# A streaming decode kernel: the last three K pieces moved up the load order, x added in mid-run, eight output-weight blocks in two ring slots

## The chip, the cores and the metric

One core of one Trainium2 chip. The metric is device time in microseconds of one execution. Times of one kernel agree to about 0.3 us in most runs, with a run about 1 us longer now and then. The profile is one execution, taken by the hardware profiler; its span is about 1.7 us shorter than the time of the same execution. MB of a single load are 1024 KB; totals and GB/s are in millions and billions of bytes, as the page gives them.

## The reference

For four requests (B = 4, one token each): attention over a cache of 8192 keys and values in 32 heads of 128, then the output weight `wo`; beside it a gated feed-forward layer of the same x; and a mix of both.

```python
x = A_x                                                   # (4, 1, 1024), bf16
g = sigmoid((x * gate_w).sum(-1, keepdims=True))
a = softmax((x @ wq -> heads) @ K^T / sqrt(128)) @ V @ wo  # K, V: (4, 32, 8192, 128)
b = x + (silu(x @ w_gate) * (x @ w_up)) @ w_down * sigmoid(x @ w_r)
return g * a + (1 - g) * b
```

K and V are 537 of the 576 MB that have to be read; every byte is used once.

## The kernel before

K and V come in 64 pieces each of 4 MB (two heads of one request: 128 partitions by 32 KB). Every load, of weights too, goes through a ring of five slots of 32 KB per partition. A K piece is transposed by DVE in four parts and multiplied by PE; four K pieces make a group with one softmax; V pieces are multiplied four steps later.

```python
ring = ctx.enter_context(tc.tile_pool(name="ring", bufs=5))
def slot():
    return ring.tile([P, RING], BF, name="piece", tag="piece")
# ... cut ...
def wo_piece(g0, g1, r0=0, r1=FR):                 # one wo block: 1 MB, in a slot of 4 MB
    ng, nr = g1 - g0, r1 - r0
    w = slot()[:, :ng * nr * D].rearrange("p (g r n) -> p g r n", g=ng, r=nr)
    nc.sync.dma_start(out=w..., in_=wov[:, g0:g1, r0:r1]...)
    def use(): ...                                 # 8 matmuls of 4x512 into acc
    return use
# ... cut ...
for u in range(NT + LAG):                          # NT = 64, LAG = 4
    if u < NT:
        k_piece(u)                                 # after every fourth: softmax(group)
    if u >= LAG:
        v_piece(u - LAG)                           # the last one is loaded in four parts
    if side:
        side.pop(0)()
    if u == NT:
        o_rows(0, GE)
        add_x()                                    # loads x again, adds (1 - g) * x
    if u == NT + LAG - 2:
        for g in range(2):
            wo_piece(g, g + 1)()
last = [wo_piece(g, g + 1) for g in range(2, NWB - 1)]
last += [wo_piece(NWB - 1, NWB, 0, FR - 1), wo_piece(NWB - 1, NWB, FR - 1, FR)]
flush()
o_rows(GE, NWB)
for use in last:
    use()
# ... then acc is cast by DVE and ACT, in halves, and stored
```

So the loads end with: V 62, wo0, wo1, V 63 in four parts of 1 MB, wo2 to wo6 (1 MB each), wo7 as 768 KB and 256 KB.

Of the kernel before, what the change touches and what calls it, by code (L numbers as in the profile page):

```python
# [19 lines left out]
def kernel(  # L20
# [22 lines left out]
    nc = tc.nc  # L43
    P = 128
    Bn, Sq, D = A_x.shape
# [6 lines left out]
    GT = 4  # L52
# [4 lines left out]
    NT = Bn * H // HT  # L57
    LAG = 4
    FR = 4
    FG = F // (P * FR)  # L60
    NB = 512
    NH = D // NB
# [18 lines left out]
    def slot():  # L81
        return ring.tile([P, RING], BF, name="piece", tag="piece")
# [53 lines left out]
    LT = const.tile([P, FR, H // FR, Bn], BF)  # L136
# [10 lines left out]
    acc = accp.tile([Bn, D], F32)  # L147

    def mm_acc(out_ap, lhsT, rhs, start=False):
        nc.tensor.matmul(out_ap, lhsT=lhsT, rhs=rhs, start=start, stop=True, skip_group_check=True)  # L150
# [15 lines left out]
    def add_x():  # L166
        xb = ptp.tile([Bn, D], BF, name="xb", bufs=1)
        nc.sync.dma_start(out=xb[:], in_=x2)
        xf = ptp.tile([Bn, D], F32, name="xf", bufs=1)
        nc.vector.tensor_copy(out=xf[:], in_=xb[:])  # L170
        for n in range(NH):
            mm_acc(acc[:, n * NB:(n + 1) * NB], dg[:], xf[:, n * NB:(n + 1) * NB])
# [6 lines left out]
    wov = A_wo.rearrange("(g p r) n -> p g r n", p=P, r=FR)  # L179
# [17 lines left out]
    def gu_piece(view, w_i, t0):  # L197
        w = slot()[:, :TW * F].rearrange("p (t g f r) -> p t g f r", t=TW, g=FG, r=FR)
        nc.sync.dma_start(out=w.rearrange("p t g f r -> p t (g f r)"), in_=view[:, t0:t0 + TW, :])
        for t in range(TW):  # L200
            for g in range(FG):
                for r in range(FR):
                    mm_acc(gu_ps[:, w_i, g, r, :], w[:, t, g, :, r], xT[t0 + t])

    def h_done():
        g_sb = stat.tile([P, FT, Bn], F32, tag="g_sb", bufs=1)
        fl = lambda ap: ap.rearrange("p g r b -> p (g r) b")
        nc.scalar.activation(out=g_sb[:], in_=fl(gu_ps[:, 0]), func=ACT.Silu)
        nc.vector.tensor_tensor(out=g_sb[:], in0=g_sb[:], in1=fl(gu_ps[:, 1]), op=ALU.mult)
        nc.vector.tensor_tensor(out=fl(hT[:]), in0=g_sb[:],  # L210
                                in1=c12[:, 1:2, :].to_broadcast([P, FT, Bn]), op=ALU.mult)

    def wd_piece(g0, ng):
        w = slot()[:, :ng * FR * D].rearrange("p (g r n) -> p g r n", g=ng, r=FR)
        nc.sync.dma_start(out=w.rearrange("p g r n -> p g (r n)"),
                          in_=wdv[:, g0:g0 + ng].rearrange("f g r n -> f g (r n)"))
        for g in range(ng):
            for r in range(FR):
                for n in range(NH):
                    mm_acc(acc[:, n * NB:(n + 1) * NB], hT[:, g0 + g, r, :], w[:, g, r, n * NB:(n + 1) * NB],  # L220
                           start=(g0 + g + r == 0))

    WB = P * FR // Dh
    NWB = H // WB
# [8 lines left out]
                                 rhs=OT[:, WB * g0 + k:WB * g1:WB, :], start=True, stop=True, skip_group_check=True)  # L233
        nc.vector.tensor_copy(out=LT[:, :, g0:g1, :], in_=lp[:])

    def wo_piece(g0, g1, r0=0, r1=FR):
        ng, nr = g1 - g0, r1 - r0
        w = slot()[:, :ng * nr * D].rearrange("p (g r n) -> p g r n", g=ng, r=nr)
        nc.sync.dma_start(out=w.rearrange("p g r n -> p g (r n)"),
                          in_=wov[:, g0:g1, r0:r1].rearrange("p g r n -> p g (r n)"))  # L240

        def use():
            for g in range(ng):
                for r in range(nr):
                    for n in range(NH):
                        mm_acc(acc[:, n * NB:(n + 1) * NB], LT[:, r0 + r, g0 + g, :], w[:, g, r, n * NB:(n + 1) * NB])
        return use


# [4 lines left out]
    def flush():  # L254
        while pending:
            pending.pop(0)()

    def heads(u):
        return divmod(u * HT, H)

    def kv_view(cache, u):
        b, h0 = heads(u)
        return cache[b, h0:h0 + HT].rearrange("h (r j) d -> (h r) (j d)", j=JR)

    def k_piece(u):
        b, h0 = heads(u)
        g, t = divmod(u, GT)
        Z = Zt[u % 2]
        for a in range(NQ):
            nc.gpsimd.tensor_copy(out=Z[32 * a:32 * a + 32, :, 31 + 32 * a:32 + 32 * a],  # L270
                                  in_=qa[32 * a:32 * a + 32, :, h0 + a // QH, b:b + 1])
        if t == 0:
            S_ps[g] = scp.tile([P, 512], F32, name="S_ps")
        sps = S_ps[g]
        kn = slot()
        nc.sync.dma_start(out=kn[:], in_=kv_view(A_k_cache, u))
        for c in range(JR // CJ):
            T = ttp.tile([P, CJ, 2, 32, 2], BF, name="T", tag="T")
            nc.vector.transpose(out=T[:].rearrange("p j h i e -> p (j h i e)").bitcast(U32),  # L279
                                in_=kn[:, c * CJ * Dh:(c + 1) * CJ * Dh].bitcast(U32))  # L280
            for jl in range(CJ // 16):
                jc = c * (CJ // 16) + jl
                s = 31 - (JC * t + jc)
                for he in range(4):
                    half, e = divmod(he, 2)
                    nc.tensor.matmul(sps[:, :], lhsT=Z[:, he, s:s + P], rhs=T[:, 16 * jl:16 * jl + 16, half, :, e],  # L286
                                     start=(t == 0 and jc == 0 and he == 0),
                                     stop=(t == GT - 1 and jc == JC - 1 and he == 3))
            if c == 0:
                flush()  # L290
        if t == GT - 1:
            softmax(g)
# [34 lines left out]
    def v_piece(u):  # L327
        b, h0 = heads(u)
        g, t = divmod(u, GT)
        B_ = PB[g % 2]  # L330
        vn = slot()
        vv = kv_view(A_v_cache, u)
        cut = 4 if u == NT - 1 else 1
        for c in range(cut):
            lo, hi = c * RING // cut, (c + 1) * RING // cut
            nc.sync.dma_start(out=vn[:, lo:hi], in_=vv[:, lo:hi])
        o_ps = ops.tile([P, 4 * Dh], F32, name="o_ps")
        n = 0
        for jc in range(JC):
            for uq in range(4):  # L340
                j0 = 16 * jc + 4 * uq
                nc.tensor.matmul(o_ps[32 * t:32 * t + NM, :], lhsT=B_[:, JC * t + jc, uq].rearrange("p s j -> p (s j)"),  # L342
                                 rhs=vn[:, j0 * Dh:(j0 + 4) * Dh], start=(n == 0), stop=(n == JR // 4 - 1))
                n += 1
                if n == 8:
                    flush()
        o_sb = OS[g % 2]
        nc.scalar.copy(out=o_sb[32 * t:32 * t + NM, :], in_=o_ps[32 * t:32 * t + NM, :])  # L348
        if t < GT - 1:
            return  # L350

        def finish():
            oT = o2p.tile([P, GH], F32, name="oT")
            for q in range(4):
                nc.tensor.matmul(oT[:, :], lhsT=o_sb[:, q * Dh:(q + 1) * Dh],  # L355
                                 rhs=selg[:, q].rearrange("p t s -> p (t s)"), start=(q == 0), stop=(q == 3))
            hg = h0 + HT - GH
            nc.vector.scalar_tensor_tensor(out=OT[:, hg:hg + GH, b], in0=oT[:, :], scalar=sgb[:, 1, b:b + 1],  # L358
                                           in1=rinv_t.pop(g)[:], op0=ALU.mult, op1=ALU.mult)
        pending.append(finish)  # L360
# [6 lines left out]
    side = [lambda: gu_piece(wgv, 0, 0), lambda: gu_piece(wgv, 0, TW), lambda: gu_piece(wuv, 1, 0),  # L367
            lambda: (gu_piece(wuv, 1, TW), h_done()), lambda: wd_piece(0, 4), lambda: wd_piece(4, FG - 4)]
    GE = NWB - GH // WB
    for u in range(NT + LAG):  # L370
        if u < NT:
            k_piece(u)
        if u >= LAG:
            v_piece(u - LAG)
        if side:
            side.pop(0)()
        if u == NT:
            o_rows(0, GE)
            add_x()
        if u == NT + LAG - 2:  # L380
            for g in range(2):
                wo_piece(g, g + 1)()
    last = [wo_piece(g, g + 1) for g in range(2, NWB - 1)]
    last += [wo_piece(NWB - 1, NWB, 0, FR - 1), wo_piece(NWB - 1, NWB, FR - 1, FR)]
    flush()
    o_rows(GE, NWB)
    for use in last:
# [36 lines left out]
```

## Time and profile before

| | before |
|---|---|
| median of 4 runs (lowest, highest), us | 1351.43 (1351.25, 1352.2) |
| profiled span, us | 1349.4 |
| loaded, MB | 576 |
| last landing mark of all loads, us from the span's start | 1345.19 |

The first lines of the page of the kernel before, with its queues: the span, busy time per engine, the packets, and for each queue its packets, MB, and share of the sixteen load engines' time.

```profile
span 1349.4 us, 11817 instructions
PE 1065.0 (79%) x5112; PEld 434.1 (32%) x5112; DVE 622.4 (46%) x403; ACT 71.0 (5%) x118; POOL 86.2 (6%) x326
DMA packets 22040, 576.46 MB, mean 427 GB/s; under 512 B 2386, under 2 KB 2394, under 8 KB 2660
...
q1 hardware_dynamic: 21968, 575.69, 99.4%
q8 instruction: 40, 0.66, 0.2%
```

No compute engine is near its limit, while the loads run at 427 GB/s over the whole span.

The table of stretches of the kernel before. Columns: the stretch, its length, busy time of each engine, granted PE clock, mean busy share of the load engines, GB/s.

```profile
core 0: us, PE busy (x) PEld busy (x) DVE busy (x) ACT busy (x) POOL busy (x), PEclk, DMA share, GB/s
60.00:1240.00 1180.00, 944.75 (x4230) 379.64 (x4230) 571.15 (x361) 61.20 (x103) 73.57 (x285) 0.91 1.00 431
...
1320.00:1336.00 16.00, 14.80 (x95) 6.48 (x94) 0.42 (x2) 1.15 (x2) 0.00 (x0) 1.00 1.00 408
1336.00:1340.00 4.00, 3.67 (x17) 1.36 (x16) 0.00 (x0) 0.00 (x0) 0.00 (x0) 1.00 0.85 327
1340.00:1346.00 6.00, 5.18 (x23) 1.93 (x23) 0.00 (x0) 0.00 (x0) 0.00 (x0) 1.00 0.48 194
```

For 1180 us the load engines are busy all the time. In the last ten the rate falls to less than half. The chain of waits is followed back from the end (start, us, what):

```profile
1309.47 20.69 DMA piece<-in_A_v_cache_dram
...
1330.21 1.90 PE o_ps L342 x8
...
1332.13 10.53 DMA piece<-in_A_wo_dram
...
1342.69 1.89 PE acc L150 x8
```

It says: the last V matmuls end at 1332.1, only then wo6 is issued (its slot was V 63's), it lands 10.5 us later, and the kernel ends after it. The timeline of the sync engine's queue confirms the late issues, and the list of its waits says why the last V piece was late too, and that the wo loads waited for V matmuls to free their slots (start, us, instruction; in the second fence: us in total, times, longest):

```profile
1308.15 1.75 SPq L336 DMA_DIRECT2D piece<-in_A_v_cache_dram  x4
...
1332.13 0.33 SPq L239 DMA_DIRECT2D piece<-in_A_wo_dram  x1
...
1336.24 2.06 SPq L239 DMA_DIRECT2D piece<-in_A_wo_dram  x2
```

```profile
SPq L239 <- PE o_ps L342: 23.2, 4, 8.6
...
SPq L336 <- PE o_ps L232: 12.4, 1, 12.4
```

The V matmuls of the last group were held by its softmax, on the timeline by the copy of the weights on POOL:

```profile
1299.37 8.75 PE L342 MATMUL o_ps<-piece,PB_143 128*8 128x512 bf16 x32 [2.11 <-POOL PB_143 L316]
```

When a load completes, the trace holds sixteen increments of its semaphore. The Trainium skill, page "DMA: Bandwidth & Descriptors", section "Why a DMA increments its semaphore by 16 and not by 1", explains them: each engine that takes part posts its own +1 behind its own data. So the first mark shows the engine that is furthest ahead, the last mark the one that is furthest behind, and only the last one ends the load. The following is worked out from the trace's landing records, in us (for the semaphores whose marks can be assigned to their loads without doubt):

```
kernel before    issued    first mark   last mark   spread
w_gate, 1st half   2.54       40.35       42.18      1.83
V, mid-run       701.05      734.12      739.04      4.92
V              1231.73     1258.65     1266.64      7.99
wo1            1295.51     1312.18     1320.22      8.04
V 63, part 1   1308.15     1314.67     1322.70      8.03
V 63, part 2   1308.53     1317.16     1325.18      8.02
V 63, part 3   1309.01     1319.65     1327.67      8.02
wo5            1325.77     1332.64     1340.17      7.53
wo6            1332.13     1336.48     1342.65      6.17
wo7, 768 KB    1336.24     1340.65     1344.55      3.89
wo7, 256 KB    1337.97     1341.31     1345.19      3.88
```

The engine that is last takes 2.47 to 2.57 us for each MB from 1320.22 to 1342.65 (nine MB in 22.43 us: 2.49 each), then 1.90 us for 768 KB and 0.64 us for 256 KB. There is no gap in its work: the pace is the same before and after the late issues. (The marks don't name the engines, so the last mark need not always be of the same one.) The engines that are ahead do run dry, which is the hole in the table of stretches.

### The profile page before, as it was taken

What the parts mean: (1) busy time and instruction counts of PE and PEld (TensorE: products, weight loads), DVE (VectorE), ACT (ScalarE), POOL (GpSimd) and SP (SyncE); (2) the same over time, 40 slices, a digit from 0 to 9 for tenths busy, and PEclk for the clock granted to TensorE, in tenths of its full rate; (3) what the DMA queues carried; (4) which work ended last, traced back from release to release, by engine and by line L of the source; (5) the groups of instructions that cost most, each with busy time, mean ns of one, the idle gap of its engine ahead of it and who ended that gap; (6) DMA issues with size and microseconds to landing.
All of it is one profiled execution on the core that took longest, in us unless ns stands there. A gap on an engine that the chain in (4) does not pass through costs nothing.

```text
span 1349.4 us, 11817 instructions
## 1 busy us (share of the span) xinstructions
PE 1065.0 (79%) x5112; PEld 434.1 (32%) x5112; DVE 622.4 (46%) x403; ACT 71.0 (5%) x118; POOL 86.2 (6%) x326
## 2 busy tenths in 40 slices
PE   2776887778788877868788777879778787887798
PEld 2432333233233323323333323333333333333333
DVE  1553445544544545355355535534553454455420
ACT  0001000000000000000000000000000000000000
POOL 2000000000000000000000000000000000000000
PEclk9877998989899888989989898999988889998999
DMA  9999999999999999999999999999999999999997
GB/s 402 431 433 422 432 431 430 431 432 433 430 431 432 431 428 432 434 430 428 432 434 431 428 432 434 431 429 430 434 431 428 432 434 432 429 429 434 433 421 321
DMA packets 22040, 576.46 MB, mean 427 GB/s; under 512 B 2386, under 2 KB 2394, under 8 KB 2660
## 3 DMA queue, kind: packets, MB, share of 16 engines
q1 hardware_dynamic: 21968, 575.69, 99.4%
q8 instruction: 40, 0.66, 0.2%
q14 instruction: 12, 0.10, 0.0%
q10 hardware_dynamic: 20, 0.02, 0.0%
HBM read 575.69 MB, written 0.01 MB: 427 GB/s over the span
## 4 chain that ended last, share of the span: by engine, by line
DMA 47%; PE 31%; DVE 11%; issue 8%; POOL 2%; ACT 1%; SPq 0%; DVEq 0%; ACTq 0%
DMA piece<-in_A_k_cache_dram 45%; PE o_ps L342 16%; PE S_ps L286 12%; DVE T L279 10%; DMA piece<-in_A_v_cache_dram 2%; PE oT L355 1%; PE acc L150 1%; DMA piece<-in_A_wo_dram 1%; DVE PT L311 1%; POOL PB_143 L316 1%; POOL PB_142 L316 1%; PE shr L150 1%; POOL tot L320 0%; ACT OS_138 L348 0%; ACT OS_139 L348 0%
## 5 line engine op out<-in xcount | busy, mean ns | idle before, releaser
L279 DVE STREAM_TRANSPOSE T<-piece 128x2048 uint32<-128x2048 uint32 x256 | 576.3, 2288 | 477.0 <-DMA piece<-in_A_k_cache_dram 395.1
L286 PE MATMUL S_ps<-T,Z_140 128*128 128x512 bf16 x1024 | 296.5, 447 | 169.0 <-DVE T L279 168.6
L286 PE MATMUL S_ps<-T,Z_141 128*128 128x512 bf16 x1024 | 253.6, 393 | 77.8 <-DVE T L279 77.7
L342 PE MATMUL o_ps<-piece,PB_143 128*8 128x512 bf16 x1024 | 227.1, 381 | 2.3 <-POOL PB_143 L316 2.1
L342 PE MATMUL o_ps<-piece,PB_142 128*8 128x512 bf16 x1024 | 226.2, 379 | 0.0
L286 PEld LDWEIGHTS <-Z_140 128*128 128x128 bf16 x1024 | 113.5, 111 | 347.8 <-issue 272.2
L286 PEld LDWEIGHTS <-Z_141 128*128 128x128 bf16 x1024 | 100.7, 99 | 229.5 <-issue 130.4
L342 PEld LDWEIGHTS <-PB_143 128*8 128x8 bf16 x1024 | 86.5, 87 | 139.8 <-issue 15.6
L342 PEld LDWEIGHTS <-PB_142 128*8 128x8 bf16 x1024 | 86.4, 87 | 137.3 <-issue 13.2
L358 DVE SCALAR_TENSOR_TENSOR OT<-oT,sgb,rinv 128x8 bf16<-128x8 f32 x16 | 3.8, 236 | 128.4 <-PE oT L355 128.4
L270 POOL COPY Z_140<-qa 32x4 bf16<-32x4 bf16 x128 | 24.9, 195 | 512.5 <-PE S_ps L286 497.7
L270 POOL COPY Z_141<-qa 32x4 bf16<-32x4 bf16 x128 | 24.9, 195 | 511.6 <-PE S_ps L286 506.0
L348 ACT COPY OS_138<-o_ps 8x512 f32<-8x512 f32 x32 | 18.4, 576 | 599.7 <-PE o_ps L342 599.7
L348 ACT COPY OS_139<-o_ps 8x512 f32<-8x512 f32 x32 | 18.4, 576 | 536.1 <-PE o_ps L342 536.1
L150 PE MATMUL shr<-xw,piece 128*128 128x4 bf16 x704 | 22.6, 170 | 3.5 <-DMA piece<-in_A_wq_dram 3.3
L150 PEld LDWEIGHTS <-piece 128*128 128x128 bf16 x704 | 22.6, 113 | 4.6 <-DMA piece<-in_A_wq_dram 3.4
L150 PE MATMUL acc<-piece,LT 128*4 128x512 bf16 x64 | 14.6, 378 | 1.1 <-DMA piece<-in_A_wo_dram 1.1
L322 DVE RECIPROCAL rinv<-tot 128x8 f32<-128x8 f32 x16 | 3.2, 202 | 25.5 <-POOL tot L320 25.5
L355 PE MATMUL oT<-selg,OS_139 128*128 128x8 f32 x64 | 8.5, 259 | 5.7 <-ACT OS_139 L348 5.7
L355 PE MATMUL oT<-selg,OS_138 128*128 128x8 f32 x64 | 8.5, 259 | 5.7 <-ACT OS_138 L348 5.7
L316 POOL COPY PB_143<-PT 64x512 bf16<-64x512 bf16 x8 | 8.2, 1026 | 66.0 <-DVE rex L318 66.0
L150 PE MATMUL acc<-piece,hT 128*4 128x512 bf16 x56 | 12.4, 379 | 0.0
(99 smaller groups left out, 145.1 us busy)
## 6 DMA issues: line engine op xcount, KB each, us to landing
piece<-in_A_k_cache_dram SPq DMA_DIRECT2D x64, 4096.0 KB, 37.4
piece<-in_A_v_cache_dram SPq DMA_DIRECT2D x63, 4096.0 KB, 36.5
piece<-in_A_wq_dram SPq DMA_DIRECT2D x2, 4096.0 KB, 22.8
piece<-in_B_w_gate_dram SPq DMA_DIRECT2D x2, 3584.0 KB, 39.6
piece<-in_B_w_up_dram SPq DMA_DIRECT2D x2, 3584.0 KB, 34.5
piece<-in_A_wo_dram SPq DMA_DIRECT2D x7, 1024.0 KB, 14.4
piece<-in_B_w_down_dram SPq DMA_DIRECT2D x1, 4096.0 KB, 39.4
piece<-in_A_v_cache_dram SPq DMA_DIRECT2D x4, 1024.0 KB, 16.7
```

The costliest lines, as they stand in the source:

```text
L150: nc.tensor.matmul(out_ap, lhsT=lhsT, rhs=rhs, start=start, stop=True, skip_group_check=True)
L270: nc.gpsimd.tensor_copy(out=Z[32 * a:32 * a + 32, :, 31 + 32 * a:32 + 32 * a], in_=qa[32 * a:32 * a + 32, :, h0 + a // QH, b:b + 1])
L279: nc.vector.transpose(out=T[:].rearrange("p j h i e -> p (j h i e)").bitcast(U32), in_=kn[:, c * CJ * Dh:(c + 1) * CJ * Dh].bitcast(U32))
L286: nc.tensor.matmul(sps[:, :], lhsT=Z[:, he, s:s + P], rhs=T[:, 16 * jl:16 * jl + 16, half, :, e], start=(t == 0 and jc == 0 and he == 0), ...
L311: nc.vector.transpose(out=PT[:].rearrange("p j i -> p (j i)"), in_=PTs[:])
L316: nc.gpsimd.tensor_copy(out=B_[W:P, :, :, 1, :], in_=Pv[W:P])
L322: nc.vector.reciprocal(out=rinv[:], in_=tot[:])
L342: nc.tensor.matmul(o_ps[32 * t:32 * t + NM, :], lhsT=B_[:, JC * t + jc, uq].rearrange("p s j -> p (s j)"), rhs=vn[:, j0 * Dh:(j0 + 4) * Dh ...
L348: nc.scalar.copy(out=o_sb[32 * t:32 * t + NM, :], in_=o_ps[32 * t:32 * t + NM, :])
L355: nc.tensor.matmul(oT[:, :], lhsT=o_sb[:, q * Dh:(q + 1) * Dh], rhs=selg[:, q].rearrange("p t s -> p (t s)"), start=(q == 0), stop=(q == 3))
L358: nc.vector.scalar_tensor_tensor(out=OT[:, hg:hg + GH, b], in0=oT[:, :], scalar=sgb[:, 1, b:b + 1], in1=rinv_t.pop(g)[:], op0=ALU.mult, op ...
```

## The change

Its intent: the last four K pieces are loaded in two pairs (60 with 61, 62 with 63), so the last softmax is done before the tail and the last V pieces don't wait for it; wo blocks share slots, four in each, so their loads can be issued early and the load engines never run dry; and the x load and its matmuls leave the tail.

```diff
-    def wo_piece(g0, g1, r0=0, r1=FR):
-        ...
-        w = slot()[:, :ng * nr * D]...
+    wo_home = {}
+    def wo_block(g, r0=0, r1=FR):
+        home, at = divmod(g, 4)
+        if home not in wo_home:
+            wo_home[home] = slot().rearrange("p (g r n) -> p g r n", g=4, r=FR)
+        w = wo_home[home][:, at]
         ...
-    for u in range(NT + LAG):
-        ...
+    order = []
+    for u in range(NT - GT):
+        order += [("k", u)] + [("v", u - LAG)] * (u >= LAG)
+    n0 = NT - GT - LAG
+    order += [("k", NT - 4), ("k", NT - 3), ("v", n0), ("k", NT - 2), ("k", NT - 1)]
+    order += [("v", u) for u in range(n0 + 1, NT)]
+    for kind, u in order:
+        if kind == "k":
             k_piece(u)
+        if (kind, u) == ("v", NT - 1):
+            for g in range(2):
+                wo_block(g)()
+        if kind == "v":
+            v_piece(u)
         ...
+        if (kind, u) == ("k", NT // 2):
+            add_x()
+        if (kind, u) == ("v", NT - LAG):
             o_rows(0, GE)
-            add_x()
-        if u == NT + LAG - 2: ...
+    last = [wo_block(g) for g in range(2, NWB - 1)]
+    last += [wo_block(NWB - 1, 0, FR - 1), wo_block(NWB - 1, FR - 1, FR)]
```

More of the change, by code (lines that the diff above doesn't have):

```diff
@@ L234, in o_rows @@
         nc.vector.tensor_copy(out=LT[:, :, g0:g1, :], in_=lp[:])
-    def wo_piece(g0, g1, r0=0, r1=FR):
-        ng, nr = g1 - g0, r1 - r0
-        w = slot()[:, :ng * nr * D].rearrange("p (g r n) -> p g r n", g=ng, r=nr)
-        nc.sync.dma_start(out=w.rearrange("p g r n -> p g (r n)"),
-                          in_=wov[:, g0:g1, r0:r1].rearrange("p g r n -> p g (r n)"))
+    wo_home = {}
[4 more added lines that the diff above has]
+        w = wo_home[home][:, at]
+        nc.sync.dma_start(out=w[:, r0:r1].rearrange("p r n -> p (r n)"),
+                          in_=wov[:, g, r0:r1].rearrange("p r n -> p (r n)"))
         def use():
-            for g in range(ng):
-                for r in range(nr):
-                    for n in range(NH):
-                        mm_acc(acc[:, n * NB:(n + 1) * NB], LT[:, r0 + r, g0 + g, :], w[:, g, r, n * NB:(n + 1) * NB])
+            for r in range(r0, r1):
+                for n in range(NH):
+                    mm_acc(acc[:, n * NB:(n + 1) * NB], LT[:, r, g, :], w[:, r, n * NB:(n + 1) * NB])
         return use
@@ L369 @@
     GE = NWB - GH // WB
-    for u in range(NT + LAG):
-        if u < NT:
-            k_piece(u)
-        if u >= LAG:
-            v_piece(u - LAG)
-        if side:
+    order = []
[6 more added lines that the diff above has]
+        if kind == "k":
+            k_piece(u)
+        if (kind, u) == ("v", NT - 1):
[3 more added lines that the diff above has]
+            v_piece(u)
+        if side and (kind == "v" or u < LAG):
             side.pop(0)()
-        if u == NT:
+        if (kind, u) == ("k", NT // 2):
+            add_x()
+        if (kind, u) == ("v", NT - LAG):
             o_rows(0, GE)
-            add_x()
-        if u == NT + LAG - 2:
-            for g in range(2):
-                wo_piece(g, g + 1)()
-    last = [wo_piece(g, g + 1) for g in range(2, NWB - 1)]
-    last += [wo_piece(NWB - 1, NWB, 0, FR - 1), wo_piece(NWB - 1, NWB, FR - 1, FR)]
+    last = [wo_block(g) for g in range(2, NWB - 1)]
+    last += [wo_block(NWB - 1, 0, FR - 1), wo_block(NWB - 1, FR - 1, FR)]
     flush()
```

## The prediction

> **What bounds the kernel now.** The load stream. The page gives 576.46 MB in a span of 1349.4 us; in the table of stretches the window from 60 to 1240 us has a DMA share of 1.00 at 431 GB/s, beside PE busy 945 of 1180 us and DVE 571. The Trainium skill, page "DMA: Bandwidth & Descriptors", section "Specifications", gives a fabric ceiling of 435 GB/s; the trace agrees, at 431. So only the two ends of the stream can give time back.
>
> **The tail before.** The last group's softmax ends at 1299.4 us (timeline) and holds the V matmuls that should have begun about 3.6 us sooner (their piece landed at 1295.8). That delays slot releases: the last V piece is issued at 1308.2 instead of about 12 us sooner (SP's waits: 12.4 us on PE), and the last three wo loads, each in a slot of its own, are issued only at 1332.1, 1336.2 and 1338.0. From 1336 to 1345 us only 2.5 MB move where the earlier rate would need 5.7 us: about 3 us of DMA idle. The naive forecast of the change is therefore -2 to -3 us.
>
> **Why I don't believe that.** Each transfer leaves sixteen landing marks. The same page, section "Why a DMA increments its semaphore by 16 and not by 1", says that each engine's last descriptor posts its own +1, so the spread of the marks is the spread between engines. The trace shows it: from 1.8 us at the start it grows to 8.0 us (first mark of a V piece 1258.65, last 1266.64), and stays there to 1328. What ends a load is the slowest engine. Its last marks in the tail stand at 1320.22, 1322.70, 1325.18, 1327.67, then 1340.17 (five blocks later), 1342.65, 1344.55 (768 KB) and 1345.19 (256 KB): 2.48 to 2.50 us per MB throughout, with no gap. The late issues starve only engines that are ahead: the spread shrinks to 3.9 us, while the last mark doesn't move. After it come the last matmuls (to 1346.5), the casts and the output's store: 4.2 us, unchanged.
>
> **What the change does.** Removed: the late softmax from the V stream's tail (about 10 us from the last scores to the weights, now early) and the slot waits of wo; the built order shows that wo2 and wo3, wo5 to wo7 wait for no slot. Moved: the x load (8 KB), its 0.63 us cast and four matmuls (1.9 us) go to mid-run, where PE is 80% busy. The pairs put two K pieces back to back: 4 transposes of 2.29 us, about 9.3 us with gaps, against 9.7 us per piece of stream, so the slot comes free in time; queued loads take 35 to 40 us to land, a deep reserve. Added bytes: none. On the critical path (the slowest engine's queue) lies next to nothing of all this.
>
> **Prediction.** 1351.3 us, range 1350.0 to 1352.6. Faster by over 2%: 0.005; within 2%: 0.99; slower: 0.005.
>
> **What would show it.** Right: wo6 and wo7 issued before about 1325 us; DMA in the last slices fuller; landing spread of the last wo loads near 8 us instead of 3.9, their first marks earlier and the last mark still at 1345 +-0.7 us; the V matmuls of the last group no longer released by the softmax; the stretch 60 to 1240 at 431 GB/s. Wrong: a last mark at about 1342 us (the idle was on the critical engine after all), or a gap in the last marks around the K pairs.
>
> **What would make it wrong.** A different assignment of small or instruction fetches to the slowest engine (shifts its queue by up to 1 us); PE falling behind on the doubled K pieces so that the queue drains; the last matmuls no longer hidden.

## The result and the profile after

| | before | after |
|---|---|---|
| median of 4 runs each, us | 1351.43 | 1351.24 (1351.19 to 1351.37) |
| ratio (95% interval) | | 0.9998 (0.998 to 1.0015) |
| profiled span, us | 1349.4 | 1349.5 |
| last landing mark, us | 1345.19 | 1345.28 |
| spread of the last load's marks, us | 3.88 | 7.92 |

A ratio here is the mean time of one kernel's fast runs over that of the other's of the same rounds, so it is not quite the ratio of the medians. The time is the same. (Every run below is marked correct; at the runs with left-out matmuls it is said how little that mark tells here.)

The change did in the profile what it was meant to do. The last V and wo loads are issued earlier (timeline of the sync engine's queue), and the last group's V matmuls wait for their own piece instead of the softmax:

```profile
1293.23 2.91 SPq L340 DMA_DIRECT2D piece<-in_A_v_cache_dram  x4
1305.53 22.59 SPq L244 DMA_DIRECT2D piece<-in_A_wo_dram  x7
```

```profile
1295.84 8.64 PE L346 MATMUL o_ps<-piece,PB_143 128*8 128x512 bf16 x32 [0.91 <-DMA piece<-in_A_v_cache_dram]
```

What the wo loads wait for has changed its kind: by the list of the queue's waits, most of it is now the landing of earlier loads, because the program keeps eight completion semaphores in turn and the ninth load waits for the first. wo6 was issued at 1322.81, just after the last mark of V 63's first part (1322.80).

```profile
SPq L244 <- DMA piece<-in_A_v_cache_dram: 26.4, 6, 9.5
```

The stretches after, to be read against those of before:

```profile
60.00:1240.00 1180.00, 947.14 (x4232) 379.91 (x4231) 578.63 (x364) 61.26 (x103) 73.64 (x285) 0.91 1.00 431
...
1320.00:1336.00 16.00, 14.95 (x97) 6.62 (x95) 0.43 (x2) 1.16 (x2) 0.00 (x0) 1.00 1.01 421
1336.00:1340.00 4.00, 4.00 (x21) 1.54 (x19) 0.00 (x0) 0.00 (x0) 0.00 (x0) 1.00 0.81 329
1340.00:1346.00 6.00, 5.32 (x25) 1.95 (x24) 0.00 (x0) 0.00 (x0) 0.00 (x0) 1.00 0.41 167
```

The stretch from 1320 rose from 408 to 421 GB/s: the holes of the engines in front are filled there. But they only finish sooner, and the last six microseconds are emptier than before (167 against 194 GB/s). The chain of waits has lost its V matmuls and its late issue, and still ends in the same place:

```profile
1293.23 29.56 DMA piece<-in_A_v_cache_dram
...
1322.81 19.94 DMA piece<-in_A_wo_dram
...
1342.79 3.79 PE acc L150 x16
```

wo6 now takes 19.9 us to land instead of 10.5: the issue moved by 9.3 us, the landing by 0.1. The marks, worked out as before:

```
kernel after     issued    first mark   last mark   spread
wo5            1320.34     1332.36     1340.18      7.83
wo6            1322.81     1334.85     1342.75      7.90
wo7, 768 KB    1325.30     1336.72     1344.63      7.92
wo7, 256 KB    1327.79     1337.36     1345.28      7.92
```

### The profile page after: what moved, and what is told of

Read it like the earlier page. It is cut to its first block, busy times and chain, and to the rows that moved or that the text cites. A ratio compares the mean times of both kernels' runs of the same rounds, so it can differ in the third digit from the quotient of the medians.

```text
span 1349.5 us, 11806 instructions
## 1 busy us (share of the span) xinstructions
PE 1066.2 (79%) x5112; PEld 434.1 (32%) x5112; DVE 622.5 (46%) x403; ACT 71.0 (5%) x118; POOL 86.3 (6%) x326
## 4 chain that ended last, share of the span: by engine, by line
DMA 48%; PE 32%; DVE 12%; issue 6%; POOL 2%; ACT 1%; DVEq 0%; SPq 0%; ACTq 0%
DMA piece<-in_A_k_cache_dram 42%; PE o_ps L346 16%; PE S_ps L290 14%; DVE T L283 10%; DMA piece<-in_A_v_cache_dram 5%; DMA piece<-in_A_wo_dram 1%; PE oT L359 1%; PE acc L150 1%; DVE PT L315 1%; PE shr L150 1%; POOL PB_142 L320 1%; POOL PB_143 L320 1%; POOL tot L324 0%; ACT OS_138 L352 0%; ACT OS_139 L352 0%
## 5 line engine op out<-in xcount | busy, mean ns | idle before, releaser
L313 ACT ACTIVATE PTs<-S_ps,negm 128x512 bf16<-128x512 f32 x16 | 11.0, 688 | 25.8 <-DVE negm L310 25.4
## 6 DMA issues: line engine op xcount, KB each, us to landing
piece<-in_A_wo_dram SPq DMA_DIRECT2D x7, 1024.0 KB, 19.9
```

The costliest lines, as they stand in the source:

```text
L313: nc.scalar.activation(out=PTs[:], in_=sps[:], func=ACT.Exp, bias=negm[:, 0:1], scale=scale, accum_out=rs[:, 0:1])
```

## The experiments

Theory A: the load engine with the longest queue is never idle, so the time is set by what that one engine has to move; earlier issue feeds engines that were not the limit. Rivals: B, the earlier issue does gain and another part of the change takes it back; C, the issue of the last loads sets the end, as the chain of waits seems to say; D, the spread of the engines is of no matter. A second theory, A2, came up on the way: what makes some engines late is the fetching of PE's own instructions. Its rivals: E, fetches don't matter; F, PE's time itself counts. Times and ratios are set against the kernel before, which ran again in each round (median 1351.23 or 1351.26), landing marks against the changed kernel.

### Shared slots alone

```diff
 # the kernel before, with wo_piece(g, g + 1) replaced by
+ wo_block(g)          # as in the change; order of pieces and add_x untouched
```

> The kernel before with the shared wo slots alone; K order and the x load as before. Theory A (the load engine with the longest queue never idles, so earlier issue gains nothing): 1351.3 +-0.4 us, last landing mark at 1345.2 +-0.5, spread of the last wo load back from 3.9 to about 8 us. Rival B (the earlier issue does gain 2 to 3 us and the pairs or the moved x give it back): 1348.5 to 1349.5.

Measured: 1351.22 us, ratio 0.9998 (0.9983 to 1.0013); wo6 issued at 1322.83, last mark 1345.23, spread 7.98. As theory A has it. Rival B falls for this part: the early issue alone gains nothing that the rest could take back.

### The rest without the shared slots

```diff
 # the changed kernel, with wo_block(g) replaced by
+ wo_piece(g, g + 1)   # as before: a slot each
```

> The changed kernel with the wo loads each in a slot of its own again, as before; pairs and early x kept. Theory A: 1351.3 +-0.4, the last wo loads issued at 1332 to 1338 again, spread of the last load about 4, last mark 1345.2. With the run of shared slots alone this leaves nothing for the pairs and x to give back.

Measured: 1351.23 us, ratio 1.0001 (0.9986 to 1.0016); the last loads are issued at 1332.12, 1336.24 and 1337.97 again, last mark 1345.18, spread 3.83. The pairs and the early x, taken together, cost and gain nothing either. They were not run apart from each other.

### Later issue, within the reserve and beyond it

wo2 to wo7 go round four places (then two), so each load waits for the matmuls of the block whose place it takes.

```diff
-        home, at = divmod(g, 4)
+        home, at = (0, g) if g < 2 else (1, (g - 2) % 4)      # % 2 in the second kernel
 ...
-    for use in last:
-        use()
+    while loaded:                       # four (two) are loaded ahead
+        loaded.pop(0)()
+        if last:
+            loaded.append(last.pop(0)())
```

> The changed kernel with wo2 to wo7 in four places, so that wo6 can be issued only after wo2's matmuls and wo7 after wo3's: about 1337 and 1339 us, 11 to 14 us later than in the changed kernel. Theory A: the slowest engine still has wo5 to read until 1340.2, so 1351.3 +-0.5, spread of the last marks under 4 us. Rival C (the chain of waits is right and the issue of the last loads sets the end): +8 to +14 us.

Measured: 1351.77 us (1351.31 to 1352.5), ratio 1.0003 (0.9988 to 1.0018). wo6 was issued at 1337.85, 15 us later than in the changed kernel, and its last mark is at 1342.70, against 1342.75. That is theory A to a twentieth of a microsecond, and rival C's +8 to +14 us fall. The two parts of wo7, issued at 1339.35 and 1339.78, did come later (last mark 1346.56 instead of 1345.28): all engines had emptied together at 1342.7, and one then needed about 1.5 us more than the first. So the end of the reserve had just been reached, and the median is 0.5 us up, which the interval doesn't tell from noise. (These marks are of the slowest of its four executions, 1352.5 us.)

> The same with two places: wo4 waits for wo2's matmuls (about 1336.9), wo5 for wo3's and so on. The slowest engine has only wo3 to read until 1335.2. Theory A: now it runs dry, landing gaps appear in the last marks, and the time rises by 3 to 7 us (estimate: a load issued at 1336.9 lands at about 1341, the last at about 1349.5). If this too stays at 1351.3, theory A's reserve is not the reason.

Measured: 1357.84 us (1356.75 to 1360.95), ratio 1.0051 (1.0036 to 1.0066); the profiled run took 1355.0. Now the chain of waits of this kernel is a true one, each load waiting for matmuls and landing 5 us later:

```profile
1338.10 5.49 DMA piece<-in_A_wo_dram
...
1343.63 1.47 PE acc L150 x6
...
1345.12 5.03 DMA piece<-in_A_wo_dram
...
1350.18 1.90 PE acc L150 x8
```

The last mark is at 1350.83, and the marks of wo5 lie within 0.22 us (1343.37 to 1343.59): all engines were idle before it. Late issue costs when the slowest engine runs dry, and not before.

### Moving bytes from one half of the engines to the other

```diff
+        if u in (40, 48):
+            cut = 0
+            nc.sync.dma_start(out=vn[0:112], in_=vv[0:112])
+            for p0 in (112, 120):
+                nc.sync.dma_start(out=vn[p0:p0 + 8], in_=vv[p0:p0 + 8])
```

> The changed kernel with two mid-run V pieces (40 and 48) loaded as 112 partitions plus twice 8 partitions, which by the skill's DMA page go to the lowest-numbered 8 engines: two 32 KB rows more for each of these and two fewer for the other 8 in all, 2 x 1.21 us each way. Theory A with the engines that are ahead among the low 8: time falls by 2.0 to 2.5 us. Theory A with the late engines among the low 8, or mixed: time rises by 2.0 to 2.5 us. Theory D (the engines share one limit and the spread is of no matter): 0 +-0.4.

Measured: 1395.95 us, ratio 1.0331 (1.0314 to 1.0348). A miss: +44.7 us, and no theory had it. The stretches show both pieces as holes in the load rate:

```profile
900.00:950.00 50.00, 27.07 (x108) 10.58 (x106) 16.10 (x11) 2.98 (x5) 2.21 (x6) 0.80 0.99 266
...
1050.00:1100.00 50.00, 34.57 (x144) 13.75 (x142) 22.73 (x18) 2.98 (x5) 3.37 (x11) 0.86 1.03 314
```

From 850 to 900 us the rate is 430 GB/s. In the holes the engines are as busy as ever (0.99 and 1.03) but move 266 and 314 GB/s: by the trace's packet records, some 200 packets of 32 KB at each hole took 2.0 to 4.2 us instead of 1.21. The Trainium skill, page "DMA: Bandwidth & Descriptors", section "The descriptor swizzle", says that in a transfer to 128 partitions each engine writes one memory port of its own; with 112 and 8 partitions that would no longer hold, which fits, but no run here separates it from other reasons. The run doesn't decide about the engines (nor shows on which of them the loads of 8 partitions ran); it shows only that this split is costly.

### PE's instruction fetches: more and fewer

Of the page's queue lines, q8 carries 40 packets of 16 KB. The Trainium skill, page "Runtime: NRT & Kernel Launch", section "Instruction fetch mechanics", says that instructions are fetched in blocks of 16 KiB, 256 instructions; the kernel's PE program has 9980, just short of 39 blocks, and in the runs below the number of these packets follows the length of PE's program (20 to 50). So they are PE's program; why there is a fortieth isn't explained. In the trace they come about 38 us apart in mid-run, take 1.0 to 1.1 us, and their durations repeat with a period of eight. The marks fit eight engines that are hit five times each: sorted, those of the last wo load of the changed kernel are

```
-7.92 -7.88 -7.68 -6.63 -6.17 -5.32 -4.88 -1.57 -0.37 -0.29 -0.26 -0.24 -0.21 -0.18 -0.08 0.00    (us before the last one)
```

First, idle matmuls were added to lengthen the program:

```diff
+        if u >= 8:
+            for _ in range(14):          # 23 in the second kernel
+                nc.tensor.matmul(shr[:, 400:404], lhsT=identb[:, :], rhs=identb[:, 0:4], start=True, ...)
```

> The changed kernel with 14 idle matmuls (128x4, into an unused corner of a PSUM tile) after each K piece from the 8th on: 11548 PE instructions instead of 9980. Theory A2 (the spread comes from PE's own instruction fetches, 40 packets of 16 KB that go round 8 of the 16 load engines, 5 each, about 1.5 us lost per fetch): 46 fetches, so at most 6 on one engine, +1.5 +-0.5 us, spread of the last load about 9.5. Rival E (fetches don't matter, PE is off the critical path): 0 +-0.3. Rival F (PE time itself counts): the idle matmuls' busy time, some 50 to 80 us, shows in part.

> The same with 23 idle matmuls: 12556 PE instructions, 50 fetches, so at most 7 on one engine. Theory A2: +3.0 +-0.7 us, spread about 11. Rival E: 0. Rival F: 1.6 times what the run with 14 shows, and no steps of 1.5.

Measured: 1357.22 us and 1373.78 us, ratios 1.0045 and 1.0166, with 46 and 50 fetches. A miss of the experiment: the idle matmuls depended on nothing, so the scheduling layer put them all in one lump near the start, where fetches then came 6 us apart, PE couldn't free slots, and the stream broke off. Stretch of the kernel with 23:

```profile
130.00:205.00 75.00, 68.47 (x959) 38.21 (x957) 19.79 (x9) 1.15 (x2) 1.56 (x8) 0.83 0.75 307
```

The size of the effect can't be read from these two times, but it can from their landing marks, and this is the most direct evidence for A2. The break let the engines start nearly level, and then each fetch put one more of them back. In the kernel with 14, worked out from the landing records as before, in us after the first mark of the same load:

```
last mark   fetches since   marks of the sixteen engines
            the break
179.1             1         fifteen up to 0.48, one at 1.98
198.5             2         fourteen up to 0.48, two at 1.84 and 1.97
266.5             4         twelve up to 0.48, four at 1.81 to 1.99
422.0             8         eight up to 0.90, eight at 1.73 to 2.02
501.2            10         eight up to 1.39, six at 1.73 to 2.01, two at 3.38 and 3.52
```

So a fetch puts one engine back by about 1.5 us; eight engines are hit before any is hit twice, and in this stretch the other eight don't make this step. (They have smaller delays of another kind, which no run explains: up to 1.39 us here, and one of them stands 6.35 us behind the first at the end of the changed kernel.) The end of the two runs agrees: after the break 33 fetches were left, which is four for each of eight engines and one over, and the last marks show one engine alone and the next seven 1.5 to 1.8 us (1.1 to 1.7 in the second kernel) before it.

Then fetches were taken away, with a wrong result and all loads kept. (The check doesn't notice that half or three quarters of the V matmuls are missing, so for the attention part the mark "correct" of any run here is weak evidence.)

```diff
-            for uq in range(4):
+            for uq in range(0, 4, 2):                 # every other V matmul
```

```diff
+            for uq in range(0, 1):                    # and in the second kernel, one V matmul of four
+                for he in range(0, 4, 3):             # and every other K matmul
```

> Wrong result on purpose: the changed kernel with every other V matmul left out, all loads kept: 7932 PE instructions, 32 fetches, 4 on one engine. Theory A2: -1.5 +-0.4 us, spread of the last load about 6.4. Rival E: 0 +-0.3, spread still 8.

Measured: the last mark came at 1343.75, 1.53 us earlier, and the spread was 6.49, both as expected. The time was not: 1350.87 us (1349.63 to 1351.9), -0.4 instead of -1.5. The fastest of its four runs does reach the expected time; the profiled one is the slowest. The timeline and the stretches show where the rest went. PE had less to do, and its granted clock was lower in the tail (0.66 from 1300 to 1320, 0.54 from 1336 to 1340, against 0.91 and 1.00 in the changed kernel). Over the changed kernel, this one and the next, the mid-run clock was 0.91, 0.85 and 0.70 with PE busy 947, 808 and 550 of 1180 us; that the one makes the other was not tested. The wo matmuls had become one unbroken row that waits for no load and ends at 1347.2, later than before:

```profile
1336.00:1340.00 4.00, 4.00 (x12) 1.20 (x10) 0.00 (x0) 0.00 (x0) 0.00 (x0) 0.54 0.78 315
```

> Wrong result on purpose: three of four V matmuls and half of the K matmuls left out, all loads kept: 4859 PE instructions, 20 fetches, at most 3 on one engine. Theory A2: -3.0 to -3.5 us, spread of the last load about 4 to 5. Rival E: 0 +-0.3.

Measured: 20 fetches, 1349.0 us (1348.87 to 1349.61), ratio 0.9984 (0.9968 to 1.0001); last mark 1342.96, 2.32 us earlier, spread 5.67. The direction is right, the size is not: the time is 2.2 us shorter, against 3.0 to 3.5 expected. One engine stands 0.8 us behind the next, so it may carry something more than three fetches; what that is stays open.

### The idle matmuls again, held in their place

Reading the piece's transposed tile ties them to their piece:

```diff
+        if 12 <= u < 62:
+            for _ in range(3):           # 21 in the second kernel
+                nc.tensor.matmul(shr[:, 400:404], lhsT=identb[:, :], rhs=T[:, 0, 0, 0:4, 0], start=True, ...)
```

> The changed kernel with 3 idle matmuls after each K piece from 12 to 61, held in their place by reading the piece's transposed tile: 10280 PE instructions, 300 more, one fetch more (41). Theory A2 (the load engine hit most by PE's instruction fetches sets the end): one engine of eight is hit a sixth time, the last mark moves from 1345.3 to 1346.8 and the time by +1.2 to +1.6 us; in the marks of the last load one stands alone, the next seven about 1.5 us before it. Rival E: 0 +-0.3.

Measured: 1352.56 us (1352.4 to 1352.71) against 1351.23, +1.33; ratio 1.0009 (0.9995 to 1.0023); last mark 1346.65. The page's queue line and the sorted marks of the last load:

```profile
q8 instruction: 41, 0.67, 0.2%
```

```
-9.43 -9.27 -9.26 -8.23 -7.98 -6.78 -6.56 -3.51 -1.89 -1.65 -1.59 -1.52 -1.47 -1.39 -1.32 0.00
```

One engine alone, then seven, as expected.

> The same with 21 idle matmuls per piece: 12080 PE instructions, 48 fetches, so all eight engines are hit six times. Theory A2: the same +1.2 to +1.6 us as with 41 fetches, though seven times as many instructions were added; the eight last marks lie within 0.5 us, the spread is near 9.5 us. Rival F (PE time itself counts): seven times the difference of the run with 3. If PE falls behind the stream, the load rate dips below 430 GB/s in the middle stretch, and the run doesn't decide.

Measured: 1352.9 us (1352.71 to 1353.43), +1.67; ratio 1.0012 (0.9998 to 1.0026); last mark 1346.84, only 0.19 us after that of the kernel with 41 fetches. The middle stretch kept its rate, so the run decides:

```profile
q8 instruction: 48, 0.79, 0.2%
...
60.00:1240.00 1180.00, 961.75 (x5247) 409.78 (x5246) 574.10 (x363) 61.17 (x103) 73.58 (x285) 0.92 1.00 431
```

```
-9.61 -9.45 -9.38 -8.15 -8.15 -6.99 -6.18 -3.28 -0.39 -0.31 -0.30 -0.29 -0.26 -0.12 -0.08 0.00
```

Eight engines within 0.4 us. Three hundred instructions more cost 1.3 us and 2100 more cost 1.7 us: a step, not a slope. Rivals E and F fall, and with them D: one engine that is late by one fetch moves the end of the kernel by one fetch. (The interval of the ratio takes in rare long runs. By themselves, every run of these two kernels, 1352.4 to 1353.43, lies above every run before in that round, 1351.11 to 1352.25.)

### What does lie on the path: the matmuls after the last mark

```diff
-    last += [wo_block(NWB - 1, 0, FR - 1), wo_block(NWB - 1, FR - 1, FR)]
+    last += [wo_block(NWB - 2, 0, 2), wo_block(NWB - 2, 2, FR)]
+    last += [wo_block(NWB - 1, 0, 2), wo_block(NWB - 1, 2, 3), wo_block(NWB - 1, 3, FR)]
```

> A try at what does lie on the path, after the last mark: the changed kernel with wo6 loaded in two halves and wo7 as 512, 256 and 256 KB, so that PE has less left to multiply when the last bytes come. Last mark unchanged at 1345.3; last matmul at about 1346.0 instead of 1346.6; time -0.4 to -0.6 us. If the time stays, the matmuls after the last mark were not what the casts waited for.

Measured: last mark 1345.29; the casts begin at 1345.74 instead of 1346.38 (timeline of DVE); profiled span 1349.0. Median of 5 runs 1350.88 against 1351.23 of 9, -0.35 us, a little short of what was expected; ratio 0.9999 (0.9987 to 1.0012). Three of the five runs (1350.69 to 1350.88) are below the lowest of before (1351.11), the other two are 1351.72 and 1352.03. If this version is better than both kernels, it is by 0.03%.

```profile
1345.74 0.68 DVE L402 CAST res<-acc 4x512 bf16<-4x512 f32 x1 [10.86 <-PE acc L150]
```

## Why the prediction was right

- "What bounds the kernel now. The load stream": right. 431 GB/s from 60 to 1240 us in both kernels, with PE and DVE times unchanged.
- "What ends a load is the slowest engine ... with no gap": right, and the step that carried the forecast. The marks show the same last landing (1345.19 and 1345.28). Issuing wo6 9.3 us earlier or 5.7 us later than before moved its landing by 0.1 us and less; only when the slowest engine ran dry by much, with two places, did the time rise clear of noise.
- "The naive forecast of the change is therefore -2 to -3 us": the hole exists, and the engines in front were idle in it; it was not worth anything, because the hole is not on the engine that ends the loads.
- "4.2 us, unchanged" after the last mark: right (1345.28 to 1349.5).
- "The slot comes free in time" at the K pairs: right, no dip (431 GB/s from 1240 to 1300 us in the changed kernel); and the two parts of the change run apart left nothing hidden, 1351.22 and 1351.23.
- "wo6 and wo7 issued before about 1325 us": not quite. They were issued at 1322.81, 1325.30 and 1327.79, because each waited for the landing of the load eight places earlier, a wait that was overlooked. It had no effect.
- "DMA in the last slices fuller": wrong for the very last. The stretch from 1320 to 1336 was fuller (421 for 408 GB/s), that from 1340 to 1346 emptier (167 for 194), as it must be when the engines in front finish sooner.
- "A different assignment of small or instruction fetches to the slowest engine (shifts its queue by up to 1 us)": the right worry, with too small a number. One more fetch on one engine moved the end by 1.3 us. What makes the spread, the prediction didn't know; it took the spread from the trace, which was enough because both kernels have 40 fetches.

What stays open: which eight engines fetch, what delays the other eight, why a fetch puts one back by about 1.5 us when its packet takes 1.0 to 1.1, whether bytes can be moved to the others, and what else one engine carried in the run with 20 fetches. If the load of the sixteen engines could be levelled, the mean of the sixteen marks above (they sum to -49.7 us) gives an estimate of the most to be had: 3.1 us, or 0.2%.

## What to carry to other kernels

A falling load rate at the end of a stream, and even a chain of waits that runs through a late issue, show that some engine was idle, not that the last one was. Look at the sixteen landing marks of the last loads: if the last marks follow each other at the full rate, earlier issue is worth nothing, and the reserve is as long as the slowest engine's queue. And in a kernel that lives on its loads, a long PE program is itself a load: count its fetches.

## What the Trainium skill lacked or had wrong

- "Runtime: NRT & Kernel Launch", section "Instruction fetch mechanics", calls the cost of crossing a 16 KiB boundary mostly hidden. In a kernel whose end is set by its loads it isn't, because the fetch delays the data loads: one fetch more on one load engine moved the kernel's end by 1.3 us (1351.23 to 1352.56), while seven further fetches on the other seven added 0.3 us.
- "DMA: Bandwidth & Descriptors" doesn't say that instruction fetches share these engines unevenly. Here the spread between them grew from 1.8 to 8.0 us over a run with 40 fetches, was 6.5 with 32 and 9.6 with 48; a single fetch put one engine back by about 1.5 us, and eight engines of sixteen were hit in turn.
- The same page, section "Latency and other measured facts", tells of engines 7 and 15 being slower and ties this, as a best guess, to loads issued by GpSimd. It has nothing on the case here: loads issued by the sync engine, of whose sixteen engines eight are late together (within 0.4 us of each other, 7.9 us behind the first).
- No page has a figure for loads split unevenly over the partitions within a stream: two pieces of 4 MB, each loaded as 112 + 8 + 8 partitions, cost 44.7 us together (1351.26 to 1395.95).
- "DMA: Bandwidth & Descriptors", section "Where 436 GB/s comes from", says that for transfers between HBM and SBUF the memory's limit of about 358 GB/s per core binds. With one core loading it didn't: 431 GB/s were held for 1180 us, close to the fabric ceiling of 435 that the page gives. (Its own single-core figure, 425 GB/s for a load of 16 MB, already points this way.)
